# Two mirrored-row scatters of one batch go to two memory tiles instead of one (attention and Fourier-mix kernel, one core)

## The chip, the core and the metric

The kernel runs on one core of a Trainium2 chip. A core has five engines with queues of their own, which run at the same time: TensorE (PE, matrix products), VectorE (DVE), ScalarE (ACT), GpSimd (POOL) and SyncE (SP). Each engine takes its instructions in the order written and stops at one that waits. Transfers are issued by SP and by POOL and carried out by the core's 16 DMA engines; an instruction that needs a transfer's data waits for its landing. The metric is the device time in microseconds of one execution: the median of several runs. The profile is one further execution, recorded on the chip.

## The reference

Eight batches of 448 rows. An attention with squared ReLU and no softmax gives x (448 × 768 for each batch); then the real part of a two-dimensional Fourier transform of x is added to it; the sum u is normalised by rows and goes through a feed-forward of 768 → 3072 → 768, and u is added again.

```python
scores = scale * np.matmul(q, k.transpose(0, 1, 3, 2))      # 8 batches, 12 heads, 448 x 64
attn = np.maximum(scores, 0.0) ** 2 / S
attn_out = np.matmul(attn, v)                               # -> x: 8 x 448 x 768
X = np.fft.fft(np.fft.fft(x, axis=1), axis=2)
u = x + np.real(X)
un = (u - mean(u)) / np.sqrt(var(u) + 1e-06)
out = u + np.maximum(un @ w_ch1, 0.0) @ w_ch2
```

## The kernel before

The kernel treats one batch after the other in three streams that are interleaved on the engines: attention (scores, squares, values), the Fourier mix with the normalisation (`first_tail` for batch 0, `mix` and `mix_rows` for the others), and the feed-forward (`ffn`), which works on groups of 384, 512 and then 256 rows of all batches in a row. A small planner in the kernel itself (`Streams.run`) fixes the order of all instructions on each engine before the kernel is compiled, from estimated durations. It does not see which tile a store goes to, and at run time the order is never changed: a late instruction holds all that stand behind it on its engine.

The Fourier sum is symmetric, so the kernel computes row s and row 448 − s of u together. The rows 0 to 223 of a batch are stored to the memory tile `utop[b]` in order (line 1237, by SP). The mirrored rows, 224 to 447, are made in descending order and must be turned round: GpSimd stores them to `ubot[b]` with an indirect transfer (line 1240), a scatter in which a table gives each row its place. Each batch has two such scatters, one for each half of the rows (`ch` = 0 and 1): in batch 0 and 1 the first, 128 rows, fills rows 97 to 223 of the tile and one row of padding; the second, 112 rows, fills rows 0 to 96 and some rows of padding beyond row 223. (The tile has 384 rows, so that the unused rows have a place.) A transfer that writes a memory tile waits for the landing of an earlier one that writes the same tile; this is added when the kernel is compiled, for whole tiles, whatever the rows are.

Tile names in the profile: `u` is the mirrored or plain half of u in on-chip memory, copied out of the accumulators by ACT and DVE (line 982 for batch 0); `qn`, `kn`, `vn` are loads of q, k and v for a group of four heads (line 412, POOL; three groups a batch); `w` are the weights (lines 442 and 453, POOL); `xn` is x transposed by a transfer (line 717, SP); `o` is where the final sum of 128 × 384 outputs is built: it is loaded with u from `utop` or `ubot` (line 1488, SP), the products are added (line 1511, DVE), and it goes out (line 1492, SP).

GpSimd's queue around the change, in order: loads of the first weight matrix and of v of batch 1 (groups 0 and 1), the first quarter of the second weight matrix, three normalisations of batch 0 (line 1003), the two scatters of batch 0, q and k of batch 1's last group, the other three quarters of the second weight matrix, v of that group, q, k and v of batch 2. On TensorE, q and k of batches 0 and 1 are transposed by products with an identity (line 543); for batch 1's last group these stand between products of the first feed-forward group (line 1789) and the values of attention (line 783).

The reads of the stored u are made by `outputs` (lines 1471 to 1494): for each block of 128 output rows it cuts the rows at the border between `utop` and `ubot` and issues one read for each part and each half of the columns. Batch 0 has 224 rows in `ubot`; its blocks read 32, 128 and 64 of them.

Of the kernel before, what the change touches and what calls it, by code (L numbers as in the profile page):

```python
# [9 lines left out]
FP32 = mybir.dt.float32  # L10
# [128 lines left out]
def need(eng, dur, deps=(), bufs=(), ok=None):  # L139
    return eng, dur, list(deps), list(bufs), ok  # L140
# [26 lines left out]
def kernel(  # L167
# [11 lines left out]
    D = H * Dh  # L179
    FF = moe_w_ch1.shape[1]  # L180
    R = S // 4
    HS = S // 2
# [29 lines left out]
    dram = ctx.enter_context(tc.tile_pool(name="dr", bufs=1, space=bass.MemoryType.DRAM))  # L212


    utop = [dram.tile([HS, D], FP32, name=f"utop{b}") for b in range(B)]
    UB = 384
    ubot = [dram.tile([UB, D], FP32, name=f"ubot{b}") for b in range(B)]
    ntop = [dram.tile([HS, D], BF16, name=f"ntop{b}") for b in range(B)]
    nbot = [dram.tile([UB, D], BF16, name=f"nbot{b}") for b in range(B)]

# [675 lines left out]
    def side(b, ch):  # L896

        return ch if b < ONE else 1
    BPC, BUN = Bufs(1), [Bufs(1), Bufs(1)]
    group_ready = [Cell() for _ in range(NGR)]  # L900
    u_stored = [[Cell() for _ in range(4)] for _ in range(B)]
# [219 lines left out]
    def first_stores(ch):  # L1121
        yield need("SP", 0.0, half_un[ch])
        yield need("SP", 0.0, u_done[ch] + [first_norms])
        freed = [Cell(), Cell()]
        for c, f in zip(freed, first_us[ch]):
            c.t = f[2]
        sch.add(u_store(0, ch, [f[0] for f in first_us[ch]], [f[1] for f in first_us[ch]], freed), (1, 1))

    def mix_rows(b, ch, pcs):
# [83 lines left out]
        for i in range(2):  # L1213
            sch.add(rows(i), rank)
        sch.add(u_store(b, ch, [lambda i=i: us[i] for i in range(2)], made_u, freed), (1, 1))
        if b > 1:
            sch.add(n_store(b, ch, made_un), (1, 1))
# [11 lines left out]
    def store_rows(b, ch, top, bot, us, nbytes, t, cells):  # L1229

        get = lambda u: u() if callable(u) else u
        s0, s1 = SC[ch]
        n, r0 = (s1 - s0, 0) if b < PAR else (R, 1 - ch)
        w = min(128, HS - s0) if b < PAR else R
        if top is not None:
            e = yield need("SP", 0.1, [t[0]])
            nc.sync.dma_start(out=top[s0:s0 + w, :] if b < PAR else top[ch::2, :], in_=get(us[0])[:w])
            cells[2 * ch].t = sch.dma(e, w * D * nbytes)
        e = yield need("POOL", 1.1, [t[1]])
        nc.gpsimd.indirect_dma_start(  # L1240
            out=bot, out_offset=bass.IndirectOffsetOnAxis(ap=(back if b < PAR else back2)[ch][:n], axis=0),
            in_=get(us[1])[r0:r0 + n], in_offset=None)
        cells[2 * ch + 1].t = sch.dma(e, w * D * nbytes) + 1.0

    def u_store(b, ch, us, ut, freed):
        yield from store_rows(b, ch, utop[b], ubot[b], us, 4, ut, u_stored[b])
        yield need("SP", 0.0, freed)
        for i in range(2):
            t = max(u_stored[b][2 * ch + i].t, freed[i].t)
            BU[i][side(b, ch)].free.append(t)  # L1250
            if b == ONE - 1 and ch == 0:
                u_left[i].t = t
# [199 lines left out]
    def uses():  # L1452

        at, odd, n = [], 0, 0
        for g in range(NGR):
            for c in WHOLES[g]:
                if g == 0:
                    at += [(g, c, hf, (0, 1, 2, 3, 5)[(n + hf) % 5]) for hf in range(2)]
                    n += 2
                else:  # L1460
                    at += [(g, c, hf, ((2, 5), (1, 3))[(c + g + 1) % 2][hf]) for hf in range(2)]
            for c in PAIRS[g]:
                odd = 1 if g < 3 else 1 - odd
                at += [(g, c, 0, 0), (g, c + 1, 0, 1 + odd), (g, c + 1, 1, 3 + odd), (g, c, 1, 5)]
        return at
# [5 lines left out]
    def outputs(slot):  # L1471

        for g, c, hf, at in uses():
            if at != slot:
                continue
            if slot == 4:
                yield need("SP", 0.0, [sq_left])
            t0, cs = GT[g] + c * 128, slice(hf * DH, (hf + 1) * DH)
            stored = [x for bb in range(t0 // S, (t0 + 127) // S + 1) for x in u_stored[bb]]
            e = yield need("SP", 0.1, stored + [ffn_begun[g]])  # L1480
            o = os[g, c, hf] = work.tile([128, DH], FP32, name="o", bufs=1,
                                              tag=f"sq{NSQ - 3}" if slot == 4 else f"o{slot}")
            t = t0
            while t < t0 + 128:
                bb, r = divmod(t, S)
                src, r = (utop[bb], r) if r < HS else (ubot[bb], r - HS)
                w = min(HS - r, t0 + 128 - t)
                nc.sync.dma_start(out=o[t - t0:t - t0 + w], in_=src[r:r + w, cs])
                t += w
            ot[g, c, hf].t = sch.dma(e, 128 * DH * 4)  # L1490
            e = yield need("SP", 0.1, [added[g, c, hf]])
            nc.sync.dma_start(out=rows[t0:t0 + 128, cs], in_=o)
            e = sch.dma(e, 128 * DH * 4)
            yield need("SP", 0.0, [e])
# [517 lines left out]
    with tc.manual_schedule():  # L2012
        small_constants()
        sch.engine.update(POOL=0.5, DVE=0.8)

        sch.add(loading(), (0, 4))
        sch.add(build_dft(), (0, 0.5))
        sch.add(turning((0,)), (0.05, 0.15))
        sch.add(ffns(), (4, 0))
        sch.add(mixes(), (1, 1))  # L2020
        sch.add(first_attention(), (0, 0))
        for i in range(2):
            sch.add(first_channels(i, range(MC - 1)), (5, 5))
        sch.add(attentions(), (3, 3))
        sch.add(warming(), (9, 9))
        sch.add(weight_sums(), (6, 6))
        sch.add(quarter_sums(), (6, 6))
        sch.add(halve(), (3, 3))
        sch.add(turns(), (1, 1))
        sch.add(turn_rest(), (2, 2))  # L2030
        sch.add(root_table(), (0, 0.4))
        sch.add(negative(), (0, 0.35))
        for slot in range(6):
            sch.add(outputs(slot), (4, 0))
        sch.fill = lambda: progress[0] > 2.0
        sch.run()
# [30 lines left out]
```

## Time and profile before

| | us |
|---|---|
| median of 3 runs (lowest, highest) | 585.75 (585.19, 587.6) |
| the profiled execution | 585.64 |
| its span, first to last instruction | 583.7 |
| TensorE busy | 567.2 (97% of the span) |
| VectorE busy | 447.4 (77%) |
| ScalarE busy | 336.6 (58%) |
| GpSimd busy | 133.1 (23%) |
| mean granted clock of TensorE | 0.994 of full |

How the lines are read: the slices of the page are 40 equal parts of the span (14.6 us), each digit the busy share in tenths. A line of the timeline has start, duration, engine, line and operation, output and inputs, how many, and in brackets how long the engine had stood idle before it and what ended that. The chain of waits follows the last instruction back to whatever released it, step by step; "issue" there is time in which the engine waited for nothing that the profile shows. A line of waits has the engine and what waited, what it waited for, total microseconds, times, and the longest. A line of windows has the stretch and its length, then busy time and instructions (x) of PE, PE's weight loads, DVE, ACT and POOL, the granted clock, the share of the DMA engines (over 1 when two queues overlap) and GB/s. The DMA lines by queue have packets, megabytes and share; queue 0 is GpSimd's, queue 1 SP's.

### The profile page before, as it was taken

Reading aid. Unit: us, or ns where it says so; the run is one execution under the profiler, and the core shown is the slowest. Engines: PE = TensorE matmul, PEld = TensorE weight load, DVE = VectorE, ACT = ScalarE, POOL = GpSimd, SP = SyncE. Lnnn points to the kernel's source line nnn. Section 1 sums busy time; section 2 is a strip of 40 time slices with the busy share of each in tenths; the row PEclk is TensorE's granted clock in tenths of the full one; section 3 lists DMA queues with packets and bytes.
Section 4 is the critical chain, followed back from the end, with each engine's and each line's share of the span. In section 5 each row is a group of like instructions: output and inputs, shape, how many; then the busy total and the mean of one; then the engine's idle time right before and its main releaser. Section 6 shows DMA issues by size and latency. Waiting matters only on the chain.

```text
span 583.7 us, 11336 instructions
## 1 busy us (share of the span) xinstructions
PE 567.2 (97%) x4339; PEld 359.2 (62%) x4344; DVE 447.4 (77%) x1030; ACT 336.6 (58%) x538; POOL 133.1 (23%) x187
## 2 busy tenths in 40 slices
PE   8999599999999999999999999999999999999997
PEld 6465356554455546545856667558567686868864
DVE  6988365987578977897899779978987994167872
ACT  5977374667664667686658757766574161405500
POOL 8523401411115211241124105212220230000000
PEclk9999799999999999999999999999999999999999
DMA  9998999866976998499959996896663343223012
GB/s 128 206 210 192 170 214 191 184 131 84 155 97 192 172 173 154 104 180 186 155 122 189 209 145 158 141 177 124 144 129 79 93 157 92 69 68 96 2 40 95
DMA packets 133493, 81.84 MB, mean 140 GB/s; under 512 B 77504, under 2 KB 128704, under 8 KB 133440
## 3 DMA queue, kind: packets, MB, share of 16 engines
q0 software_dynamic: 40320, 33.63, 37.1%
q1 hardware_dynamic: 93120, 47.50, 36.9%
q8 instruction: 34, 0.56, 0.4%
q14 instruction: 19, 0.16, 0.1%
HBM read 62.91 MB, written 26.25 MB: 153 GB/s over the span
## 4 chain that ended last, share of the span: by engine, by line
PE 83%; DVE 9%; DMA 4%; ACT 2%; issue 1%; POOL 0%; SPq 0%; DVEq 0%; POOLq 0%; ACTq 0%
PE psF L1789 29%; PE psF L1929 21%; PE psS L855 6%; PE psF L783 4%; PE psF L1817 4%; PE psS L1929 4%; PE psS L1631 3%; PE psF L1844 3%; PE psS L1330 2%; DVE sq L885 2%; DMA ubot<-u,back 2%; DMA qkT<-qkr 1%; PE psS L783 1%; ACT sq L868 1%; PE psS L2007 1%; DMA qn<-in_q_dram 1%
## 5 line engine op out<-in xcount | busy, mean ns | idle before, releaser
L1789 PE MATMUL psF<-unT,w 128*128 128x256 bf16 (+2 forms) x1435 | 199.4, 295 | 1.1 <-ACT hT L1776 0.7
L868 ACT ACTIVATE sq<-psS 112x896 bf16<-112x896 f32 x192 | 165.1, 930 | 40.4 <-PE psS L855 40.1
L1789 PEld LDWEIGHTS <-w 128*128 128x128 bf16 x1440 | 138.0, 98 | 59.4 <-issue 14.0
L1776 ACT ACTIVATE hT<-psF 128x512 bf16<-128x512 f32 (+3 forms) x144 | 71.6, 513 | 73.9 <-PE psF L1789 72.8
L885 DVE TENSOR_TENSOR sq<-sq 112x896 bf16<-112x896 bf16 x163 | 98.5, 621 | 16.0 <-ACT sq L868 15.1
L1929 PEld LDWEIGHTS <-hT 128*128 128x128 bf16 x720 | 69.0, 98 | 50.4 <-issue 5.9
L1929 PE MATMUL psF<-w,hT 128*128 128x384 bf16 x378 | 67.1, 326 | 0.7 <-DVE xT L610 0.7
L1511 DVE TENSOR_TENSOR o<-psF,o 128x384 f32<-128x384 f32 x80 | 44.3, 553 | 26.1 <-PE psF L1929 20.8
L855 PE MATMUL psS<-qkT 64*128 64x448 bf16 (+1 forms) x384 | 52.6, 358 | 2.4 <-ACT sq L868 1.9
L412 POOL DMA_DIRECT2D vn<-in_v_dram x24 | 17.6, 732 | 107.2 <-PE psS L855 86.1
L1174 POOL TENSOR_TENSOR u<-tp,xn 112x385 f32<-112x385 f32 (+2 forms) x14 | 13.6, 972 | 107.3 <-DVE tp L1156 80.1
L855 PEld LDWEIGHTS <-qkT 64*128 64x128 bf16 (+1 forms) x384 | 17.3, 101 | 30.6 <-issue 24.3
L610 DVE TENSOR_SCALAR xT<-psF 128x224 bf16<-128x224 f32 x54 | 18.5, 384 | 22.7 <-PE psF L783 22.6
L783 PE MATMUL psF<-sq,vn 112*64 112x448 bf16 x264 | 31.3, 358 | 0.9 <-DVE hT L1774 0.9
L1202 ACT ACTIVATE un<-u,nmr,rstd 113x768 bf16<-113x768 f32 (+2 forms) x23 | 23.1, 1023 | 14.9 <-DVE nmr L1189 13.2
L412 POOL DMA_DIRECT2D qn<-in_q_dram x21 | 15.2, 723 | 62.7 <-DVE qkr L507 53.0
L1183 DVE BATCH_NORM_STATS2 stats<-u 112x6 f32<-112x384 f32 (+2 forms) x56 | 28.8, 541 | 0.0
L1929 PE MATMUL psF<-wsum,hT 128*128 128x384 bf16 x162 | 28.8, 326 | 0.0
L1774 DVE TENSOR_SCALAR hT<-psF 128x512 bf16<-128x512 f32 (+3 forms) x36 | 20.6, 583 | 10.3 <-PE psF L1789 9.8
L783 PEld LDWEIGHTS <-vn 112*64 112x64 bf16 x336 | 15.8, 109 | 19.6 <-issue 12.9
L882 ACT ACTIVATE sq<-sq 112x896 bf16<-112x896 bf16 x29 | 27.4, 952 | 0.5
L1817 PE MATMUL psF<-w,hT 128*128 128x384 bf16 x144 | 24.9, 326 | 0.0
(227 smaller groups left out, 787.5 us busy)
## 6 DMA issues: line engine op xcount, KB each, us to landing
out_dram<-o SPq DMA_DIRECT2D x56, 192.0 KB, 3.1
vn<-in_v_dram POOLq DMA_DIRECT2D x24, 224.0 KB, 5.4
qn<-in_q_dram POOLq DMA_DIRECT2D x21, 224.0 KB, 4.6
kn<-in_k_dram POOLq DMA_DIRECT2D x21, 224.0 KB, 7.0
w<-in_moe_w_ch_dram POOLq DMA_DIRECT2D x12, 384.0 KB, 11.8
w<-in_moe_w_ch_dram POOLq DMA_DIRECT2D x4, 1152.0 KB
utop<-u SPq DMA_DIRECT2D x12, 336.0 KB, 3.0
o<-utop SPq DMA_DIRECT2D x16, 192.0 KB, 5.9
```

The costliest lines, as they stand in the source:

```text
L412: nc.gpsimd.dma_start(out=t, in_=src[b, hs].rearrange("h (p j) d -> p h (j d)", j=4))
L783: nc.tensor.matmul(av[h * Dh:(h + 1) * Dh, 0:S], lhsT=vn[:, c, h0 + h, :], rhs=sq[:, h, :], start=(c == 0), stop=(c == 3))
L855: nc.tensor.matmul(sc[:wide, h, 0:S].rearrange("k (c q) -> k c q", c=4), lhsT=flat[ps, k0:k0 + wide], rhs=qT[ps, m % 2], start=True, stop= ...
L868: nc.scalar.activation(r, sc[:R, :, 0:S], AF.Relu)
L882: nc.scalar.activation(r, r, AF.Square)
L885: nc.vector.tensor_tensor(r, r, r, op=ALU.mult)
L1183: nc.vector.bn_stats(stats[:n, hf, :], u[:n, hf * (D // 2):(hf + 1) * (D // 2)])
L1511: nc.vector.tensor_tensor(o, pc[:, 0:DH], o, op=ALU.add)
L1776: nc.scalar.activation(hs, ps, AF.Relu)
L1789: nc.tensor.matmul(ph[:, i * N:(i + 1) * N], lhsT=w1_sb[m][hf][:, (jj + i) * 128:(jj + i + 1) * 128], rhs=unT[:, m, 0:N], start=(m == 0), ...
L1817: nc.tensor.matmul(pc[:, 0:DH], lhsT=block(j, c), rhs=w2(j, hf), start=(j == 0), stop=(j == JC - 1))
L1929: nc.tensor.matmul(pc[:, 0:DH], lhsT=lhs[i], rhs=rhs[i], start=(start and i == 0), stop=(i == KP - 1), skip_group_check=True)
```

## The change

Batch 0's second scatter goes to a memory tile of its own, `ulow`, of the same size as `ubot[0]`. The reads of batch 0's lower rows take rows 0 to 96 from `ulow` and rows 97 to 223 from `ubot[0]`; a block that reaches over row 97 is read in two parts. The other batches are as before. The planner's input, and with it the order of the instructions on the engines, stays the same, but for two reads more on SP: the block of 128 rows, read once for each half of the columns, becomes 65 and 63 rows.

```diff
     ubot = [dram.tile([UB, D], FP32, name=f"ubot{b}") for b in range(B)]
+    ulow = dram.tile([UB, D], FP32, name="ulow")
...
     def u_store(b, ch, us, ut, freed):
-        yield from store_rows(b, ch, utop[b], ubot[b], us, 4, ut, u_stored[b])
+        yield from store_rows(b, ch, utop[b], ulow if b == 0 and ch else ubot[b], us, 4, ut, u_stored[b])
...
                 bb, r = divmod(t, S)
-                src, r = (utop[bb], r) if r < HS else (ubot[bb], r - HS)
-                w = min(HS - r, t0 + 128 - t)
+                src, r, last = (utop[bb], r, HS) if r < HS else (ubot[bb], r - HS, HS)
+                if bb == 0 and src is ubot[0] and r < HS - 127:
+                    src, last = ulow, HS - 127
+                w = min(last - r, t0 + 128 - t)
                 nc.sync.dma_start(out=o[t - t0:t - t0 + w], in_=src[r:r + w, cs])
                 t += w
```

## The prediction

> **What bounds the kernel now.** I began with the page: busy times and the forty slices.
>
> ```profile
> PE 567.2 (97%) x4339; PEld 359.2 (62%) x4344; DVE 447.4 (77%) x1030; ACT 336.6 (58%) x538; POOL 133.1 (23%) x187
> ...
> PE   8999599999999999999999999999999999999997
> ...
> PEclk9999799999999999999999999999999999999999
> ```
>
> TensorE is the bound: 97% busy, and after the start only one slice of forty has a hole (the 5, a slice of 14.6 us from 58.4 us on). The same slice has the only dip of the clock that the throttle granted. So whatever the change is worth must be looked for there, and time won on other engines elsewhere is worth nothing. The waits of TensorE name the hole, and its timeline places it.
>
> ```profile
> PE psF L543 <- DMA qn<-in_q_dram: 5.3, 1, 5.3
> ...
> 57.52 0.78 PE L855 MATMUL psS<-qkT 64*112 64x448 bf16 x6
> 63.56 0.58 PE L543 MATMUL psF<-ident,qn 112*64 112x112 bf16 x8 [5.26 <-DMA qn<-in_q_dram]
> ```
>
> TensorE was done at 57.52 + 0.78 = 58.30 and stood until 63.56: the transposes of q of batch 1's last group had no data. Next comes the chain of waits from 45 to 72 us, which says why q was late.
>
> ```profile
> 46.27 8.94 DMA ubot<-u,back
> ...
> 56.09 0.35 POOL ubot L1240
> 56.45 0.64 issue
> 57.08 6.43 DMA qn<-in_q_dram
> ...
> 63.56 0.58 PE psF L543 x6
> 64.14 2.05 PE psF L1789 x6
> ...
> 66.21 0.57 DVE hT L1774
> ...
> 66.82 2.04 PE psF L1789 x6
> ...
> 68.88 0.50 ACT hT L1776
> ...
> 69.42 0.58 PE psF L543 x16
> ...
> 71.47 4.01 PE psF L1789 x24
> ```
>
> Read it upwards from TensorE: q was issued at 57.08 and landed at 63.51; it was issued only then because GpSimd's queue stood at the second scatter (56.09), and this stood until the first scatter had landed (46.27 + 8.94 = 55.21). That is the wait the change removes. From 69.42 on the chain is TensorE nearly without a break, so a microsecond won before it moves the end by one, as long as nothing else becomes late.
>
> **The change part by part.** *The second scatter's wait.* Compiled, the second scatter no longer waits for the first one's landing; it keeps its waits for the copies that make its u tile and for a weight load eight transfers earlier in GpSimd's queue, which lies ahead of the first scatter there and cannot hold it past that scatter's own landing. The last transposes of the group whose q buffer is used again, and the copies:
>
> ```profile
> 49.01 0.39 PE L543 MATMUL psF<-ident,qn 112*64 112x112 bf16 x8
> ...
> 48.47 0.49 ACT L982 COPY u<-psF 112x384 f32<-112x384 f32 x1
> 48.60 0.55 DVE L982 COPY u<-psF 112x384 f32<-112x384 f32 x1
> ...
> 56.09 0.98 POOL L1240 DMA_INDIRECT ubot<-u,back  x1 [8.71 <-ACT hT L1776]
> 57.08 0.80 POOL L412 DMA_DIRECT2D qn<-in_q_dram  x1
> ...
> 58.61 2.51 POOL L453 DMA_DIRECT2D w<-in_moe_w_ch_dram  x3
> ```
>
> They end at 49.15, so the scatter can go at about 49.4 instead of 56.09, q at 50.4, k behind it, the three weight loads from 52 on: all some 6.7 us earlier. q's buffer is free by then: the transposes that read it last ended at 49.40.
>
> *When q lands.* The transfers of GpSimd's queue still stand behind the first scatter. What the DMA engines did meanwhile, by windows (the columns after the clock are the DMA share and GB/s):
>
> ```profile
> 50.00:52.00 2.00, 1.81 (x39) 1.26 (x38) 1.62 (x3) 2.00 (x3) 0.00 (x0) 1.00 1.17 215
> 53.00:54.00 1.00, 1.00 (x7) 0.53 (x7) 0.90 (x3) 1.00 (x3) 0.00 (x0) 1.00 0.59 186
> 54.00:55.00 1.00, 0.92 (x6) 0.43 (x5) 1.00 (x3) 0.83 (x2) 0.00 (x0) 1.00 0.12 49
> 56.00:57.00 1.00, 1.00 (x9) 0.45 (x8) 1.00 (x2) 0.57 (x2) 0.91 (x1) 1.00 0.00 0
> 61.00:62.00 1.00, 0.00 (x0) 0.00 (x0) 0.00 (x0) 0.00 (x0) 1.00 (x3) 0.91 1.29 160
> 62.00:63.00 1.00, 0.00 (x0) 0.00 (x0) 0.00 (x0) 0.00 (x0) 1.00 (x2) 0.50 2.35 203
> 68.00:70.00 2.00, 1.42 (x21) 0.79 (x21) 0.37 (x1) 0.49 (x1) 0.00 (x0) 0.84 1.16 211
> ```
>
> From 53 on the engines ran dry and were idle until the second scatter came. With it and q already queued they go on at once. Best end: q lands right after the first scatter, 55.2, and TensorE does not wait. Worst end: it takes its 6.43 us again from 55.21 on, 61.6, and 3.3 us of the stall remain. Between them: the second scatter (112 rows of 3 KB, 0.34 MB) and q (0.23 MB) at 215 GB/s are 2.7 us; from about 54, with 0.8 us from the last bytes to the landing (about 54.4 to 55.2 for the first scatter) and up to 1 us for engines that finish late, that is 57.5 to 58.5. TensorE needs q at 58.30. I charge 0.4 us of rest. k follows 1.1 us later (0.23 MB) and is needed 1.3 us after q (the first transposes and six products): nothing. Gain: 5.26 − 0.4 = 4.9 us.
>
> *The clock.* The windows show it full until 61, half from about 61.9 on, 3.5 us into the stall, and full again at about 68.6 (0.84 over 68 to 70). A rest of 0.4 us does not get that far. In the chain the pieces of TensorE at half clock are 0.58 + 2.05 + 2.04; at full clock six products take 4.01 / 4 = 1.00 and eight transposes 0.58 / 2 = 0.29, together 2.29. The evictions between them (0.57 and 0.50) stay. Gain: 4.67 − 2.29 = 2.4 us. The Trainium skill (TensorE: Matmul & The Clock Gate, part 1 on the clock gate) says that about 3.4 us of idleness halve the clock and about 3.4 us of work restore it; the first agrees with the 3.5 here, while here the return took 5.1 us from 63.56. By the page's figure the half-speed stretch would cost only 1.7 us, an estimate, and the time below would come out 0.7 us later.
>
> *What is late next.* TensorE would be 7.3 us ahead from there. The load it then nears is v of the same group, issued behind the weights.
>
> ```profile
> 89.34 0.95 PE L783 MATMUL psF<-sq,vn 112*64 112x448 bf16 x8
> ...
> 71.06 0.71 POOL L412 DMA_DIRECT2D vn<-in_v_dram  x1 [7.83 <-PE psF L783]
> ...
> DMA to landing us min/median/max: 21.8/21.8/21.8
> ...
> q0 software_dynamic: 475, 0.73, 99.6%
> q0 software_dynamic: 682, 0.39, 70.4%
> ```
>
> The second and third lines are v of the next group, issued at 71.06 and so landed at 92.9; the last two are GpSimd's queue in 78 to 82 and 82 to 86 us (packets, MB, share). Three loads of 0.23 MB lie between the two v's, at 0.10 to 0.18 MB/us 4 to 7 us; so our v landed at 86 to 89, say 87, some 2.3 us before its use at 89.34. With the change it is wanted at 82.0. The queue gains the idle stretch from about 54.4 to beyond 57, some 3.5 us, and about one of the slow restart after it, say 4.7. But the drop from 0.73 to 0.39 MB comes from the loads of u on SP's queue, which follow TensorE and so come 7.3 us earlier, into v's way rather than after it: I take some 0.4 us of it. v lands at 82.7 then: 0.7 us given back. Bounds: nothing (landing before 82.0) to 2.6 us (landing at 89.3 now, gain 4.7).
>
> *The wait that moves.* A later q load (batch 2) now carries the wait for the first scatter, at 55.2; it stands behind the three weight loads and v in the queue, so it cannot go before 54.5 anyway; behind it are k of batch 2 and the v at 71.06, which waits for TensorE. Nothing.
>
> *Two more reads on SP.* Two reads of 128 rows of u become 65 + 63 rows each: two issues more. SP's transfers take eight counters in turn and each waits for the transfer eight places before, so the two shift who waits for whom.
>
> ```profile
> 78.40 1.52 SPq L1488 DMA_DIRECT2D o<-utop  x3
> 79.97 0.42 SPq L1488 DMA_DIRECT2D o<-ubot  x1
> 85.50 6.79 SPq L717 DMA_TRANSPOSE xn<-xT  x2
> ...
> o<-utop SPq DMA_DIRECT2D x2, 144.0 KB, 8.3
> ...
> 105.75 0.92 POOL L1174 TENSOR_TENSOR u<-tp,xn 128x385 f32<-128x385 f32 x1 [7.90 <-DVE tp L1156]
> ```
>
> 0.42 us each on a queue that mostly waits. The transpose issued at 85.50 now stands behind a read of u issued at 78.4 that can need 8.3 us, until 86.7: 1.2 us later. Its result is first read at 105.75, and that reader waited for something else. Nothing; without this cover it would be at most 2 us.
>
> *Sum.* 4.9 + 2.4 − 0.7 = 6.6 us off the profiled execution's 585.64 (span 583.7, 1.9 around it): 579.0. The median of the runs, 585.75, is 0.1 above that execution, which changes nothing; 0.5%, 2.9 us, is about what a measurement tells from no change.
>
> **The rivals.** *q still comes late.* The worst end above: 3.3 us of stall remain. If the clock holds, the gain is 5.3 − 3.3 + 2.4 = 4.4 (and v is in time): 581.3; if it halves once more, 2.0: 583.7. For it: with the second scatter gone ahead, q took 6.43 us on engines that had just stood idle. Against: the engines were idle before, and are not now.
>
> *Nothing changes.* The second scatter's own row calls its releaser an eviction of ScalarE (hT, L1776), not a DMA. If the scatter truly waits for ScalarE to get there, it goes at 56 as before: 585.6. Against it: its u was copied at 48.96 and 49.15, and the chain runs through the landing at 55.21.
>
> *The stall moves to v and the kernel gets slower.* GpSimd's queue gains nothing, since SP's transposes and reads fill what it won; v lands at 87.0 as now, TensorE waits from 82.0, 5.0 us, over 3.5, so the clock halves again (2.4): all is given back, 585.7. Later than 87.0, the kernel is slower: if the fall from 0.73 to 0.39 MB in 4 us (0.34 of 0.73, 1.9 us lost) comes a second time ahead of v, v lands at 88.9 and the time is 587.6. For it: that this fall is there. The Trainium skill (DMA: Bandwidth & Descriptors, Queues, rings and completion order) has each DMA engine take turns between the queues with work, packet by packet; that fall agrees. Against: 3 us of idle DMA engines are closed whatever comes after.
>
> **How the numbers follow.** Forecast 0.70, q late 0.14, nothing changes 0.08, slower 0.05, others 0.03. The forecast's own range goes from 578.0 (no rest, v in time) to 580.9 (no rest, 2.6 at v). The range of 8 in 10 reaches into the late q, to 583.0, and 0.6 below 578.0 for the scatter of runs. Faster by 0.5% means under 582.8: the forecast, most of the late q and some of the others, 0.86; same 0.08; slower 0.06.
>
> **What would show it.** The second scatter at 49 to 50.5 on GpSimd, q issued right behind; no idle DMA at 55 to 57; TensorE's wait for q below 1 us; the clock at 1.00 in every window from 58 to 70; the 24 products of 71.47 beginning near 64; any new wait at the use of v near 82. Wrong would be a scatter still at 56, a landing of q after 60, or a wait for v over 3 us.

## The result and the profile after

The changed kernel takes 579.2 us (median of 4 runs) against 585.85 for the kernel before, measured beside it: ratio 0.9873, 95% interval 0.9839 to 0.9908; by the medians it is 6.6 us less. The profiled execution took 579.77 us, its span is 577.7. (In some executions, by its mean clock of 0.977 also in one of these four, 587.92 us, TensorE runs at half clock from about 14 us to 42 us or later; the ratios leave out those over 1.5% above the fastest of their kernel, and without that one the median of the changed kernel is 578.6, 7.2 us less.)

The page after: busy times, TensorE's forty slices and the clock.

```profile
PE 565.3 (98%) x4339; PEld 358.7 (62%) x4344; DVE 446.8 (77%) x1030; ACT 337.0 (58%) x538; POOL 133.3 (23%) x187
...
PE   8999999999999999999999999999999999999997
...
PEclk9999999999999999999999999999999999999999
```

The hole of the fifth slice and the dip of the clock are gone, and the DMA engines no longer stand idle from 55 to 57 us (their share is the last number but one):

```profile
55.00:56.00 1.00, 0.51 (x4) 0.32 (x4) 1.00 (x1) 1.00 (x2) 1.00 (x2) 1.00 1.10 175
56.00:57.00 1.00, 1.00 (x10) 0.47 (x10) 1.00 (x2) 0.57 (x2) 0.73 (x2) 1.00 1.29 175
```

GpSimd's timeline shows why:

```profile
46.33 1.11 POOL L1241 DMA_INDIRECT ubot<-u,back  x1 [0.17 <-issue]
50.01 1.41 POOL L1241 DMA_INDIRECT ulow<-u,back  x1 [2.56 <-ACT sq L869]
51.42 0.80 POOL L413 DMA_DIRECT2D qn<-in_q_dram  x1
...
55.40 0.76 POOL L413 DMA_DIRECT2D vn<-in_v_dram  x1
56.44 0.71 POOL L413 DMA_DIRECT2D qn<-in_q_dram  x1 [0.27 <-issue]
57.23 0.70 POOL L413 DMA_DIRECT2D kn<-in_k_dram  x1
```

The second scatter goes at 50.01 instead of 56.09, q at 51.42 instead of 57.08, and all that stands behind them comes 5 to 6 us earlier too: the last two rows are q and k of batch 2. TensorE's timeline:

```profile
58.13 0.39 PE L544 MATMUL psF<-ident,qn 112*64 112x112 bf16 x8
...
63.94 4.07 PE L1792 MATMUL psF<-unT,w 128*128 128x384 bf16 x24
...
83.06 0.95 PE L784 MATMUL psF<-sq,vn 112*64 112x448 bf16 x8 [1.11 <-DMA vn<-in_v_dram]
...
102.62 0.36 PE L856 MATMUL psS<-qkT 64*128 64x448 bf16 x2 [0.34 <-DVE qs L1159]
```

The rows of before, from its timeline, that answer to the 24 products, to q and k of batch 2 on GpSimd and to the copy of k further below:

```profile
61.77 0.76 POOL L412 DMA_DIRECT2D qn<-in_q_dram  x1
62.47 0.76 POOL L412 DMA_DIRECT2D kn<-in_k_dram  x1
...
71.40 4.07 PE L1789 MATMUL psF<-unT,w 128*128 128x384 bf16 x24
...
104.30 0.43 DVE L507 COPY qkr<-kn 112x1024 bf16<-112x1024 bf16 x1 [0.52 <-DMA qkT<-qkr]
```

At 58.13 no idle time stands behind the row: q is there. Against before TensorE is 63.56 − 58.13 = 5.4 us ahead there, 71.40 − 63.94 = 7.5 at the 24 products, 89.34 − 83.06 = 6.3 after a wait for v, and the spans differ by 583.7 − 577.7 = 6.0. So two small waits, 1.11 and 0.34 us, give back some 1.5 us of 7.5. The chain of waits after names what both waited for, and a row of VectorE's timeline belongs to the second:

```profile
55.40 27.61 DMA vn<-in_v_dram
...
92.61 7.31 DMA qkT<-qkr
100.02 0.43 DVE qkr L508
100.44 0.48 DVE tp L1157
...
102.62 0.36 PE psS L856 x2
```

```profile
100.02 0.43 DVE L508 COPY qkr<-kn 112x1024 bf16<-112x1024 bf16 x1 [2.51 <-DMA qkT<-qkr]
```

The second is no load of q's kind: from batch 2 on, VectorE copies q and k into order (`qkr`, line 508) and a transfer of SP turns them (`qkT`). VectorE stood 2.51 us at the copy of the second group's k, until the transfer that reads the same buffer for the first group had landed, so the four sums of batch 1's mix behind it (`tp`, `qs`) were late, and with them the memory that TensorE's scores need.

### The profile page after: what moved, and what is told of

It reads as the page before. It is cut to its first block, busy times and chain, and to the rows that moved or that the text cites. A ratio compares the mean times of both kernels' runs of the same rounds, so it can differ in the third digit from the quotient of the medians.

```text
span 577.7 us, 11341 instructions
## 1 busy us (share of the span) xinstructions
PE 565.3 (98%) x4339; PEld 358.7 (62%) x4344; DVE 446.8 (77%) x1030; ACT 337.0 (58%) x538; POOL 133.3 (23%) x187
## 4 chain that ended last, share of the span: by engine, by line
PE 80%; DVE 7%; DMA 6%; ACT 4%; issue 1%; POOL 1%; SPq 0%; DVEq 0%; ACTq 0%
PE psF L1792 28%; PE psF L1932 21%; PE psS L856 5%; DMA vn<-in_v_dram 5%; PE psF L784 4%; PE psS L1932 4%; PE psS L1634 3%; PE psF L1847 3%; ACT sq L869 3%; PE psF L1820 3%; PE psS L1331 2%; DMA qkT<-qkr 1%; PE psS L784 1%; PE psS L2010 1%; PE psF L1634 1%
## 5 line engine op out<-in xcount | busy, mean ns | idle before, releaser
L1932 PEld LDWEIGHTS <-hT 128*128 128x128 bf16 x720 | 69.0, 98 | 50.4 <-issue 5.9
L1932 PE MATMUL psF<-w,hT 128*128 128x384 bf16 x378 | 67.1, 326 | 0.7 <-DVE xT L611 0.7
L1820 PE MATMUL psF<-w,hT 128*128 128x384 bf16 x144 | 24.9, 326 | 0.0
L1847 PE MATMUL psF<-w,hT 128*128 128x384 bf16 x144 | 24.4, 326 | 0.0
```

The costliest lines, as they stand in the source:

```text
L1820: nc.tensor.matmul(pc[:, 0:DH], lhsT=block(j, c), rhs=w2(j, hf), start=(j == 0), stop=(j == JC - 1))
L1847: nc.tensor.matmul(pc[:, 0:DH], lhsT=block(2 * i + k, c), rhs=weights[i], start=(start and i == 0), stop=(i == KP - 1), skip_group_check=True)
L1932: nc.tensor.matmul(pc[:, 0:DH], lhsT=lhs[i], rhs=rhs[i], start=(start and i == 0), stop=(i == KP - 1), skip_group_check=True)
```

## The experiments

**The same kernel again.**

> The changed kernel once more, beside the others on one chip. Expected 577.7 to 579.8 as before; TensorE waits under 0.3 us for q near 58 and 0.5 to 1.5 us for v near 83, clock 1.00 throughout.

579.21 (577.38 to 586.85), ratio 0.9879 (0.9839 to 0.992). The result stands. The execution that was profiled is the one of 586.85, in which TensorE comes to q only at 66.7 us; the two waits that were expected can't be checked in it.

**The cut reads alone.** One tile as before, but the block of 128 rows is read as 65 and 63:

```diff
+                if bb == 0 and src is ubot[0] and r < HS - 127:
+                    last = HS - 127
```

> The kernel before with one tile, but the reads of batch 0's 128 lower rows cut into 65 and 63 rows as in the changed kernel. Theory: two issues of 0.4 us more on a queue that mostly waits cost nothing: 585 to 586. Rival (the smaller reads or the shifted counters of SP's queue bring a part of the gain or cost one): more than 1.5 us from 585.8.

585.46 (584.88 to 587.32), ratio 0.9995 (0.9978 to 1.0013). The two reads more on SP cost nothing that can be measured.

**Later again, by 33 and by 66 small instructions.** With the tile of its own, GpSimd rewrites an index table that it already has, with the same values, ahead of the second scatter:

```diff
+        for _ in range(33 if bot is ulow else 0):        # 66 in the other
+            nc.gpsimd.iota(back2[1], pattern=[[0, 1]], base=HS - 1, channel_multiplier=-2)
         nc.gpsimd.indirect_dma_start(
```

> The changed kernel with 33 small instructions on GpSimd ahead of the second scatter (index tables written again with the same values), some 3 us, so that q is issued near 54 instead of 51.4. Theory (until the first scatter's bytes are through near 54, an earlier issue is worth nothing, since the queue keeps its order): q lands less than 2 us later than in the changed kernel, near 59 to 60, the stall is 1 to 2 us and the clock holds: 579 to 581. Rival (what counts is the time of the issue alone): 3 us of delay cost 3 us, 582 or more.

> The same with 66 instructions, some 6 us: q is issued near 57, as in the kernel before. Theory: the stall is back at about 5 us, the clock halves again, and the time is that of the kernel before, 585 to 586, although the tiles are two and no wait on a landing is left. Rival (the two tiles help otherwise): clearly under 585.

582.84 (582.39 to 585.02), ratio 0.993 (0.9905 to 0.9954), and 589.89 (589.07 to 599.66), ratio 1.0046 (1.0023 to 1.007). Timelines, first with 33, then with 66 (both traces begin about 0.7 us earlier than that of before):

```profile
46.73 6.46 POOL L1242 IOTA backe<- 128x1 int32 x33
53.82 1.01 POOL L1243 DMA_INDIRECT ulow<-u,back  x1 [0.64 <-ACT sq L869]
54.83 0.80 POOL L413 DMA_DIRECT2D qn<-in_q_dram  x1
...
60.90 0.39 PE L544 MATMUL psF<-ident,qn 112*64 112x112 bf16 x8 [3.44 <-DMA qn<-in_q_dram]
```

```profile
46.73 12.97 POOL L1242 IOTA backe<- 128x1 int32 x66
60.34 1.00 POOL L1243 DMA_INDIRECT ulow<-u,back  x1 [0.64 <-ACT sq L869]
61.34 0.81 POOL L413 DMA_DIRECT2D qn<-in_q_dram  x1
...
67.41 0.59 PE L544 MATMUL psF<-ident,qn 112*64 112x112 bf16 x8 [9.96 <-DMA qn<-in_q_dram]
```

The instructions took 6.5 and 13.0 us, more than was planned, so the times lie above those of the theory that leaves room before q is late; the first reaches its rival, the time of issue alone, but with this longer delay it doesn't part the two. Allowing for the time lines, the second scatter is 4.5 and 11.1 us later than in the change, and the medians are 3.6 and 10.7 us above its median. The rows show the same: TensorE starts on q 60.90 − 53.82 = 7.08 and 67.41 − 60.34 = 7.07 us after the second scatter's issue. In the kernel before, with the landing wait, it is 63.56 − 56.09 = 7.47. With a tile of its own but the scatter at 60.34, the kernel is slower than before. So the tile of its own gains by the earlier issue that it allows; of another gain nothing is seen.

**The clock alone.** The kernel before, with 30 idle products in the stall; they write an accumulator that is overwritten and are no part of the output:

```diff
+                    for _ in range(30 if b == 1 and g == NG - 1 and r == 0 else 0):
+                        nc.tensor.matmul(ptf[:, 0:384], lhsT=w1_sb[0][0][:, 0:128], rhs=groups[0][2][:, 0, 0:384],
+                                         start=True, stop=True)
```

> The kernel before, with 30 idle products (128 x 384, results overwritten) on TensorE in the place of the stall at 58.3, ahead of the transposes that wait for q: 30 x 0.163 = 4.9 us of work in 5.26 us of stall. Nothing arrives sooner, so this isolates the clock. Theory: the clock stays at 1.00, the transposes still begin near 63.5, and the 2.4 us of half-speed work go: 583.2, between 582.5 and 584. If the clock has no part in the gain: 585.6; if it follows its own rhythm and not the idleness: half speed somewhere near all the same.

586.15 (584.45 to 587.17), ratio 0.9991 (0.997 to 1.0013): no gain. The timeline, and two waits:

```profile
57.98 5.05 PE L542 MATMUL psF<-unT,w 128*128 128x384 bf16 x30
64.69 0.39 PE L546 MATMUL psF<-ident,qn 112*64 112x112 bf16 x8 [1.66 <-DMA qn<-in_q_dram]
...
68.52 0.39 PE L546 MATMUL psF<-ident,qn 112*64 112x112 bf16 x8 [0.58 <-ACT hT L1779]
```

```profile
PE psS L1333 <- DVE fold L704: 1.4, 1, 1.4
...
PE psS L858 <- DVE qs L1161: 0.6, 1, 0.6
```

The clock stayed full here, and from q's first transposes to the second ones it is 68.52 − 64.69 = 3.83 us where before has 69.42 − 63.56 = 5.86: the clock was worth 2.0 us there. But q came 1.1 us later in this execution, mostly because the second scatter did (56.79 against 56.09). The 0.9 us of lead left at 68.52 were lost at the scores of batch 2, in the wait of 0.6 us (the products behind it begin at 108.60, in before at 108.69); in the other wait, at 170 us, VectorE again stood at a copy of k behind a transposition, and TensorE fell 1.4 us behind. So a lead of TensorE alone was worth nothing in the kernel before, by the medians and by this trace, and that had not been expected. That it was lost because the later loads were not earlier is a reading that the trace suggests (q and k of batch 2 went 0.9 us later here than in before) and the next kernels test.

**One tile, the loads ahead of the scatter.** The second scatter keeps its wait for the landing, but q and k of batch 1's last group are issued ahead of it:

```diff
             loads[i][x] = t.rearrange("p h (j d) -> p j h d", j=4)
+            if i == NG + 2 and x == 1:
+                held_back.pop()()          # the second scatter of batch 0
```

> The kernel before with one tile and the wait for the first scatter's landing kept, but the second scatter is issued after q and k of batch 1's last group instead of ahead of them. Theory (all that matters is when q is issued on GpSimd's queue): q is issued near 47.5, right behind the first scatter, and the time is that of the changed kernel or up to 1 us less, 578 to 580; GpSimd still stands at the second scatter until 55.2, and the weight loads are issued as late as before, near 57 to 60, so v may land up to 2 us later than in the changed kernel. Rival (the separate tiles themselves help, since the stores and the reads of u no longer wait for one another): 585 to 586, no change, as the tile is one and the wait is there.

586.06 (584.85 to 590.6), ratio 0.9993 (0.9968 to 1.0018): nothing, where the whole gain was expected. A second look was taken.

> The version with q and k ahead of the second scatter and one tile, once more, for a profile whose start runs at full clock: its time was that of the kernel before, where the theory of the queue had expected the changed kernel's. Either q lands near 58 and the time is lost later (then a wait of over 3.4 us with half clock stands at the use of v near 82, as the weights and v were issued behind the scatter again), or the stall at 58 is still there (then q was held by something that the changed kernel does not have: its landing is after 60 although it was issued before 51).

589.52. In neither trace does TensorE come to q before 68 us, when q has long landed, so they don't show where the lead goes. The next step moves v ahead too (`x == 2`, and v's load in front of the three weight loads):

> One memory tile as before, but q, k and v of batch 1's last group are all issued ahead of the second scatter, which then waits for the landing of the first as before; the three weight loads and q and k of batch 2 go behind it, at their times of before. It asks where the lead of the kernel with q and k alone ahead (q_first, 586.06) went. If v was late there (issued at 61 as before, landing at 86 to 89, wanted at 82, so a stall of some 5 us and a half clock), v is cured here and the time is 578 to 581. If q and k of batch 2, which stay behind the scatter and in the kernel before have no slack (the kernel with idle products lost its lead of 0.9 us on them at 108 us), take the lead, then it is lost some 20 us later: 584 to 586.5, with a wait of several us at the scores of batch 2 and once more a half clock.

584.52 (582.37 to 587.74), ratio 0.9963 (0.9939 to 0.9988). First GpSimd's timeline, then waits, chain and windows:

```profile
49.45 0.80 POOL L412 DMA_DIRECT2D qn<-in_q_dram  x1 [2.17 <-PE psF L544]
...
57.12 1.00 POOL L1241 DMA_INDIRECT ubot<-u,back  x1 [5.47 <-DVE sq L886]
...
61.32 0.74 POOL L412 DMA_DIRECT2D kn<-in_k_dram  x1
```

```profile
PE psS L856 <- DMA qkT<-qkr: 2.1, 1, 2.1
PE psS L856 <- DVE qs L1159: 1.9, 2, 1.2
```

```profile
61.32 28.41 DMA kn<-in_k_dram
...
92.82 10.41 DMA qkT<-qkr
103.33 0.43 DVE qkr L508
```

```profile
104.00:108.00 4.00, 2.43 (x10) 0.94 (x11) 3.93 (x7) 2.44 (x3) 3.64 (x4) 0.73 0.17 51
108.00:112.00 4.00, 4.00 (x23) 1.91 (x22) 3.90 (x13) 2.65 (x4) 1.42 (x2) 0.84 0.91 283
```

q and v are in time here, with no wait at 58 or at 82. But k of batch 2 still goes at 61.32, behind the waiting scatter, and lands 28.41 us later. From 101 to 106 TensorE waits 4.0 us on that path and falls to half clock (0.73 and 0.84 in the windows): 20 us later most of the lead is gone. That is the second theory, as expected. Of the 6.6 us some 2 remain by the medians, and by the spans of the profiled executions 583.7 − 582.5 = 1.2 of 6.0. So most of the change's gain hangs on the loads behind the scatter coming earlier as well. Which of them is not shown: the three weight loads and q and k of batch 2 all stay behind it here. By the rows the late landing of k is the smaller part: it is 89.73 here and 88.1 in the change, and the transposition of k is issued at 92.82 here and at 92.61 there, but takes 10.41 us instead of 7.31. What made it longer was not tested. The 1.5 us between this kernel and q_first are not clear of the noise, as the two intervals overlap. Where q_first itself waits was not seen in a trace. A wait for v is likely, since v goes behind the weights there as in the kernel with the idle products, where it landed at 61.94 + 25.7 = 87.6; but that is only argued.

**v ahead of the weights, in the changed kernel.**

```diff
-        yield from load_group(NG + 2, (0, 1))
+        yield from load_group(NG + 2)
         yield from load_w2(range(1, 4))
-        yield from load_group(NG + 2, (2,))
```

> The changed kernel, with v of batch 1's last group loaded ahead of the three weight loads instead of behind them; nothing else is moved. Theory (what the changed kernel gives back is the wait for v, 1.11 us, behind 3.5 MB of weights): the wait near 82 goes, the weights land 1 us later and are not needed before 90: 1.1 us less than the changed kernel, 577 to 578.5. Rival (the give-back lies elsewhere, or the next late transfer, the transposed q and k of batch 2, takes it back): within 0.4 us of the changed kernel.

579.05 (577.52 to 586.59), ratio 0.9847 (0.9812 to 0.9882), which can't be told from the change alone, as the rival had it. The wait for v is gone, and another is longer:

```profile
PE psS L855 <- DVE qs L1158: 1.9, 2, 1.2
```

**And the copy of k behind the sums.** In addition VectorE makes the copy of k of batch 2's second group after the four sums of batch 1's mix instead of ahead of them:

```diff
+                    if (b, g, x) == (2, 1, 1):
+                        k_held.append(copy)
+                    else:
+                        copy()
...
         ts = [qs, tp]
+        if own:
+            k_held.pop()()
```

> The changed kernel with v ahead of the weights, and on VectorE the copy of batch 2's second k (which waits for the transposition that reads its buffer, 2.5 us in the changed kernel) behind the four sums of batch 1's mix instead of ahead of them; nothing else moves. Theory (moving v alone brought nothing, because TensorE then waited up to 1.9 us for the fourth of these sums, queued behind that copy): without both waits 1 to 2 us less than the changed kernel, 576.5 to 578. Rival (the copy's delay makes the transposed k of batch 2 late in its turn): within 0.4 us of the changed kernel, or above it.

577.85 (577.22 to 578.55), ratio 0.9845 (0.9814 to 0.9876), span 576.5. TensorE's row at the scores:

```profile
100.55 0.74 PE L862 MATMUL psS<-qkT 64*128 64x448 bf16 x6 [0.27 <-DMA qkT<-qkr]
```

The waits of 1.9 us have become 0.27, so the order of VectorE's queue made them. This is the fastest kernel of the study; its interval overlaps that of the change, so the 1.3 us between the medians are not shown to be a gain.

**Batch 1's scatters separated too,** together with v ahead of the weights:

```diff
-    ulow = dram.tile([UB, D], FP32, name="ulow")
+    ulow = [dram.tile([UB, D], FP32, name=f"ulow{b}") for b in range(2)]
...
+                if bb < 2 and src is ubot[bb] and r < HS - 127:
+                    src, last = ulow[bb], HS - 127
```

> The version with v first, and the same separation of tiles for batch 1, whose second scatter stands 4.1 us for the landing of the first at 115 us. Theory: behind that scatter on GpSimd's queue stand loads that nothing on TensorE waits for, so the second separation brings nothing: the time of the version with v first, within 0.4 us. Rival (a scatter that does not wait is a gain wherever it stands): 1 us or more under it.

594.92 (593.17 to 603.38), ratio 1.0133 (1.0095 to 1.0171): some 16 us slower than with v ahead alone, where no difference was expected. A wait of TensorE, SP's timeline, and windows:

```profile
PE psS L1330 <- DVE fold L701: 13.0, 1, 13.0
```

```profile
149.44 12.00 SPq L1490 DMA_DIRECT2D o<-utop  x2
...
162.35 3.07 SPq L519 DMA_TRANSPOSE qkT<-qkr  x1
```

```profile
152.00:153.00 1.00, 1.00 (x8) 0.38 (x8) 0.00 (x0) 0.30 (x2) 0.00 (x0) 1.00 0.08 18
...
158.00:159.00 1.00, 1.00 (x9) 0.31 (x8) 0.00 (x0) 0.80 (x3) 0.00 (x0) 1.00 0.07 19
```

In batch 1 the border at row 97 leaves a read of 127 rows. SP stands 12 us, and in six of these, from 152 to 155 and from 158 to 161, the DMA engines are busy to a share of 0.07 to 0.08, about one of sixteen, at 17 to 19 GB/s. The transposed q and k behind it are late. The Trainium skill (DMA: Bandwidth & Descriptors, Why a DMA increments its semaphore by 16 and not by 1) has the number of DMA engines be the largest divisor of the rows up to 16, for 127 rows one; the windows agree. The same separation with that read cut into 112 and 15 rows (and v where the change has it):

```diff
+                w = 112 if w == 127 else w
```

> The changed kernel with batch 1's second scatter on a tile of its own too, and its reads of 127 rows cut into 112 and 15 rows. In the version that had both separations and v first, TensorE waited 13 us near 165 behind a read of 127 rows on SP's queue. Theory (the 127 rows go through very few DMA engines, 112 and 15 through 16 and 15): the wait is gone and the time is that of the changed kernel, 578 to 580, so the second separation is worth nothing. Rival (the wait comes from the separation, or from the earlier v): 590 or more again.

579.12 (578.38 to 587.17), ratio 0.9864 (0.9814 to 0.9914). SP's answering row has no such stop:

```profile
148.95 0.88 SPq L1492 DMA_DIRECT2D o<-utop  x2
```

The stop of SP and the wait of TensorE are gone with the cut, so the read was the cause (the cut was not run with v ahead, but v ahead alone has no such wait either), and separating batch 1's scatters too is worth nothing that can be measured.

## Why the prediction was right, point by point

It said 579.0; the median is 579.2 and the profiled execution took 579.77. The mechanism was right: the landing wait, the earlier issue of q, the clock, and the next wait at v. That the number meets to 0.2 us is partly luck, as the terms below show.

- *The second scatter's wait.* Predicted at about 49.4, q at 50.4; found at 50.01 and 51.42. The rival that nothing changes, because the row of before names ScalarE as the releaser, is out: the scatter went six microseconds ahead of that eviction's place, and the name was not the cause.
- *When q lands.* Charged with 0.4 us of rest; it was nothing: 5.4 us ahead at 58.13 against 4.9 predicted. q landed at 51.42 + 6.4 = 57.8, between the two ends as taken, and the working is borne out: q still stands behind the first scatter. In the change and in the four kernels built on it that issue q early (v_first, v_first_k_later, both, two_cut), q is issued 4.4 to 5.4 us before the first scatter lands and comes 2.0 us after that landing each time (in the change the first scatter lands at 55.8, the second at 56.7). Issued once the first scatter had landed, q takes 6.0 to 6.7 us: 6.4 in before, 6.0 with 66 instructions, where the engines had gone idle. So the charge of 0.4 was not needed, and that the change too has 6.4 us from issue to landing is chance.
- *The clock.* Predicted 2.4 us; TensorE won 7.5 − 5.4 = 2.0 between q and the 24 products, and the idle products show the same 2.0. The term was 0.4 too large: for six products it took a quarter of 24 products without a break, 1.00 us, where the rows of six at full clock have 1.14 to 1.15, and for eight transposes 0.29, where the row has 0.39.
- *What is late next.* The use of v, as predicted: wanted at 83.06 − 1.11 = 81.95 (predicted 82.0), and 1.1 us late instead of 0.7. Its landing before, put at 87, fits the 87.6 of the kernel with the idle products. The step left out a second place, q and k of batch 2 at 102 us, whose first wait in the change is 0.34 us and which gives back more as soon as v does not. All that was given back is about 1.5 us, twice the term. (The upper end of the forecast's own range, 580.9, is worked out with the rest of 0.4 us, though it says no rest; without it, 5.3 + 2.4 − 2.6 = 5.1 gives 580.5.)
- *The wait that moves* was called nothing, and so it is. But there the prediction passed over what mattered most: q and k of batch 2 had little room in the kernel before (VectorE stood 0.52 us at 104.30 for a transposition), and most of the gain lasts only because the change brings the loads behind the scatter 5 to 6 us earlier too. With the weights and q and k of batch 2 left behind the wait (qkv_first), some 1 to 2 of 6 to 6.6 us remain.
- *Two more reads on SP*: nothing, as the cut reads alone show.
- *Sum.* In the profiled execution it is 5.4 + 2.0 − 1.5 = 5.9 us (585.64 − 579.77) against the 6.6 predicted: 0.5 more for q, 0.4 less for the clock, 0.8 more given back. These errors partly cancel. The medians differ by the full 6.6, since this execution is 0.6 above the median of its kernel; that this makes up for the rest of the errors is chance.
- *The rivals.* q still late: no. The stall moving to v: the mechanism is real, but in the change it has a size of 1.1 us, not 5. Where only q, k and v of batch 1 get ahead and not the rest of the queue (qkv_first), a stall does eat most of the gain, at batch 2's loads.

## What to carry to other kernels

A wait in a queue delays everything behind it: list not only the load that is late now but each one behind it with its room, because a lead at the first use may be kept only if the later loads come earlier too, as here. Test such a change by moving the loads in front of the wait one after the other; the point where the lead is lost moves along and names the next one. And when rows are cut at a border, look at the counts that remain: here 127 rows held a queue for 12 us where 112 and 15 cost nothing that could be measured.

## What the runs showed of the hardware

*The clock goes by a grid of its own.* Windows with 33 and then with 66 delaying instructions (the clock is the third number from the end):

```profile
62.40:62.80 0.40, 0.37 (x8) 0.26 (x9) 0.39 (x1) 0.00 (x0) 0.00 (x0) 0.58 1.06 172
69.20:69.60 0.40, 0.40 (x4) 0.18 (x3) 0.16 (x1) 0.40 (x2) 0.40 (x1) 0.89 1.20 233
```

```profile
59.60:60.00 0.40, 0.00 (x0) 0.00 (x0) 0.00 (x0) 0.05 (x1) 0.10 (x1) 0.53 0.03 3
76.40:76.80 0.40, 0.40 (x4) 0.00 (x0) 0.36 (x3) 0.40 (x1) 0.40 (x2) 0.64 1.20 219
```

From the shares within these windows the half clock lasts from 62.46 to 69.29 (6.8 us) and from 59.62 to 76.69 (17.1 us); before, from its windows of 61 to 62 and 68 to 70, from 61.8 to 68.6 (6.8 us). In the cut reads alone, whose stall is 6.5 us, it lasts from 59.44 to 73.10 (13.7 us), by the shares of 0.80 in 59.2 to 59.6 and 0.63 in 72.8 to 73.2. These are 2, 5, 2 and 4 times 3.4 us. And with 33 instructions it begins 1.6 us after TensorE was at work again (60.90). In both delayed kernels TensorE stopped at the same 57.46 on their own time lines, yet the clock fell 5.0 us later in one and 2.2 in the other; with the cut reads, stopped at 57.46 too, it was 2.0. So "3.5 us into the stall", as the prediction read it, was chance. The clock's part of a stall differs with it: with the cut reads TensorE needs 73.37 − 63.97 = 9.40 us from q's first transposes to the 24 products, in before 7.84, in the change 5.81. The Trainium skill (TensorE: Matmul & The Clock Gate, part 1) has a window of 3413 ns that runs freely; these lengths agree with it, and the prediction had read the page as counting from the start of the idle time.

*When a load of 224 KB lands goes here by what stands ahead of it on the queue.* Issued after the first scatter's landing, with the 0.34 MB of the second one ahead, q took 6.0 to 6.7 us, on idle DMA engines too. Issued 4 to 5 us before that landing it came 2.0 us after it, and 1.1 us after it where the second scatter was not ahead (qkv_first: 56.3 and 57.4). At the 215 GB/s that the prediction used, the second scatter and q together are 2.7 us. What the rest of the 6 us is was not tested.
